# Signs for the projections in four wide instructions, a routing head in three planned pieces, float32 products in parts of two

## The chip, the core and the metric

One core of a Trainium2 chip runs the whole program. The metric is the device time of one launch in microseconds; the figure that counts is the median of several launches. TensorE is called PE here, VectorE DVE, ScalarE ACT, GpSimd POOL, and SyncE, which issues most of the DMAs, SP.

## What is computed

Three layers follow one another on 1536 tokens of width 512.

1. Attention with hashed buckets: for 2 batches of 8 heads, 768 positions of 64 numbers, the signs of `q @ proj` and `k @ proj` (six columns) give each row a bucket, and a query sees only the keys of its own bucket.
2. A mixture of 8 experts with a capacity of 192 tokens each. All (token, expert) logits are taken in falling order, and a token goes to the first expert that still has room. An expert is `relu(x @ w1) @ w2`.
3. A dense layer `silu(x @ w_in) @ w_out` with 2048 hidden columns.

```
for idx in order:                       # logits in falling order
    tok, e = idx // E, idx % E
    if assigned[tok] >= 0 or counts[e] >= cap: continue
    assigned[tok] = e; counts[e] += 1
h = maximum(x[mask] @ w1[e], 0);  out[mask] = h @ w2[e]
```

## The kernel before

**The order of the work.** The instructions of each of the two stages (attention; experts and dense layer) are not written down in their order of execution. Each step is an `op` with an engine, a modelled duration, the steps it depends on and a key; `Plan.run` (L38) then builds a list schedule. It always takes the step that can start first in its model, and among equal starts the one with the lowest key. A step may be held back if a step whose key is lower by more than `gap` would become ready before it ends (less `tol`). Two steps of one engine that depend on each other are put 0.13 us apart in the model (`SLAT`), and in the second stage a step of PE that waits for another engine is planned 0.8 us later than it could start. Every engine then runs its list strictly in that order, so an instruction that waits holds up all that stands behind it on its engine. A change of any modelled duration, or of how a step is cut, can give another order.

**The start.** `lp` (L139) loads `proj` into both halves of `p32`; `pl` (L142) splits it into a rounded part and a rest (`phi`, `plo`), adds the negated copies and puts sixteen blocks of 64 x 6 into `PL`, whose other elements POOL has set to zero (L138). `PL` is the stationary operand of the matmuls of L232, which give the bits of both q and k in one PSUM bank. The other steps of the start are the transposes of q and k (L198, PE), the rounded part of the result (L201, ACT) and the rest (L203, DVE). On POOL stand the memsets of the head buffers (L160 to L162).

**The routing.** The experts close one after another, so there are eight phases. In each, `head` of `route` (L603) finds each token's best open expert; seven calls of `count` (L573) then narrow down the logit at which the next expert is full: compare on DVE (`cmp`, L578), count on PE (`rp`, L582), compare with the room left (`ok`, L585), spread on PE (L588), reduce on DVE (L589). `fin` and `cnt` close the phase. `slots` (L698) then numbers the rows of the expert that closed: `s0` (the expert's number), `f0` (L712, ends with `tot`), `p0` on PE (`rpp`, L726), one-hot rows (`oh`, L735), matmuls that turn them into token numbers (`rpi`, L745), and a gather of 192 rows by POOL (L753) that are transposed on PE (L760). The chain of the next phase and `slots` of the phase just closed compete for the same DVE. The steps of the first four phases have keys below all others.

**The products.** The first six experts that close use their float32 weights as they come (`whole`, L812): a product of four or eight matmuls, planned as steps of four matmuls (1.28 us each in the model). The last two experts and the dense layer use rounded parts and rests (`product`, `second`). The dense layer works on groups of two experts, so its first products (L883) need both experts of the first group.

**The conversion.** The weights of the dense layer come as 64-bit words (`Weights.plan`, L452); 32 blocks are converted with one step on ACT and DVE steps `c1` (two instructions, L467 and L468, planned as one step of 0.8 us), `c2` (L469) and `c3` (L470, on POOL for half of them).

Of the kernel before, what the change touches and what calls it, by code (L numbers as in the profile page):

```python
# [97 lines left out]
def attention(ctx, tc, q, k, v, proj, wg, L, ident, xd, npairs, MW, KC):  # L98
# [34 lines left out]
    V.tensor_scalar(mag,rf[:,1:2],-BIG,1.0,op0=ALU.mult,op1=ALU.add)  # L133
    p32=c1.tile([128,6],F32,name="p32"); wgs=c1.tile([128,4,8],F32,name="wgs")

    phi=c1.tile([128,2,6],F32R,name="phi"); plo=c1.tile([128,2,6],F32R,name="plo")
    PL=c1.tile([128,2,2,128],F32R,name="PL")
    G.memset(PL.bitcast(F32),0.0)  # L138
    def lp():  # L139
        for h in range(2): nc.sync.dma_start(p32[64*h:64*h+64],proj)  # L140
# [285 lines left out]
FP = 6  # L426
# [14 lines left out]
class Weights:  # L441
# [10 lines left out]
    def plan(self, P, a, b, key, pool, ring, after=lambda m: []):  # L452

        nc=self.nc; V=nc.vector; raw={}
        for m in range(a,b):
            n,h=divmod(m,2); c=n//2
            def load(m=m,n=n,h=h,c=c):
                r=raw[m]=pool.tile([128,512,2],I32,name=ring,tag=ring)
                if n%2==0: src=self.wi[h*256:(h+1)*256,c*256:(c+1)*256].rearrange("(a p) f t -> p a (f t)",p=128)
                else: src=self.wo[c*256+h*128:c*256+h*128+128].rearrange("(a p) d t -> p a (d t)",p=128)  # L460
                nc.sync.dma_start(r.rearrange("p (a b) t -> p a (b t)",a=2-n%2),src)
            def t(n=n,h=h): return self.W[n][:,h*512:(h+1)*512]
            def c0(m=m,n=n,h=h,t=t):
                if h==0: self.W[n]=self.res.tile([128,1024],F32,name=f"w{n}")
                nc.scalar.activation(t(),raw[m][:,:,1].bitcast(F32),AF.Abs)
            def c1(t=t):
                V.tensor_scalar(t(),t(),LOW,HIGH,op0=ALU.max,op1=ALU.min)  # L467
                V.tensor_scalar(t().bitcast(I32),t().bitcast(I32),3,0x3FFFFFFF,op0=ALU.logical_shift_left,op1=ALU.bitwise_and)  # L468
            def c2(m=m,t=t): V.scalar_tensor_tensor(t().bitcast(I32),raw[m][:,:,1],-0x40000000,t().bitcast(I32),op0=ALU.bitwise_and,op1=ALU.bitwise_or)  # L469
            def c3(m=m,t=t): V.scalar_tensor_tensor(t().bitcast(I32),raw[m][:,:,0],29,t().bitcast(I32),op0=ALU.logical_shift_right,op1=ALU.bitwise_or)  # L470
            def c4(m=m): l=raw[m][:,:,0]; nc.scalar.activation(l,l.bitcast(U32),AF.Copy,scale=2.0**-29)
            def c5(m=m,t=t): nc.gpsimd.tensor_tensor(t().bitcast(I32),t().bitcast(I32),raw[m][:,:,0],op=ALU.add)
            k=key+m
            P.op(("c64",m),"SP",.45,load,after(m),k,ring,dma=2.3)
            P.op(("cv",m,0),"Activation",.53,c0,[("c64",m)]+([("cv",m-1,0)] if h else []),k)
            P.op(("cv",m,1),"DVE",.8,c1,[("cv",m,0)],k)
            P.op(("cv",m,2),"DVE",.61,c2,[("cv",m,1)],k)
            if m in C3P:
                P.op(("cv",m,4),"Activation",.53,c4,[("c64",m)],k)
                P.op(("cv",m,3),"Pool",1.35,c5,[("cv",m,2),("cv",m,4)],k,frees=[("c64",m)])  # L480
            else: P.op(("cv",m,3),"DVE",.61,c3,[("cv",m,2)],k,frees=[("c64",m)])
# [39 lines left out]
def moe(ctx, tc, L, xd, w1, w2, MW, K, ident, out):  # L521
# [78 lines left out]
    def route(ph):  # L600
        last=ph==7
        ch=Chain(("R",ph),[] if ph==0 else [T_["end",ph-1]])
        def head():  # L603
            eq=rt.tile([128,12,8],F32,name="eq",tag="eq")
            M=T_["M"]=rt.tile([128,12],F32,name="M",tag="M"); mr=rt.tile([128,12],F32,name="mr",tag="mr")
            if ph==0:
                V.tensor_scalar(Lc,L,-1e36,0.0,op0=ALU.max,op1=ALU.add); Lm=Lc
            else:
                pen=rt.tile([128,8],F32,name="pen",tag="pen")
                V.tensor_scalar(pen,T_["cnt"],CAP-0.5,NEG,op0=ALU.is_ge,op1=ALU.mult)  # L610
                Lm=rt.tile([128,12,8],F32,name="Lm",tag="Lm")
                V.tensor_tensor(Lm,Lc,b8(pen),op=ALU.add)
            V.tensor_reduce(M,Lm,axis=AX.X,op=ALU.max)
            V.tensor_tensor(eq,Lm,b12(M),op=ALU.is_equal)
# [7 lines left out]
            V.tensor_tensor(T_["Bw",ph],eq,b12(mr),op=ALU.is_equal)  # L622
        T_["Bw",ph]=None
        ch("DVE",2.7 if ph else 1.6,head)
        if not last:
# [72 lines left out]
    def slots(ph):  # L698
# [56 lines left out]
        for h in range(2):  # L755
# [12 lines left out]
            op(("xt",ph,h),"PE",.5,xt,[("g",ph,0),("g",ph,1)]+([("w1",ph-2,7,1 if ph-2>=FP else 0)] if ph>1 else []),rk(ph)+h*.01,"rp")  # L768
            op(("xh",ph,h),"Activation",.38,xh,[("xt",ph,h)],rk(ph)+h*.01,frees=[("xt",ph,h)])
# [42 lines left out]
    def whole(nm,u,w,xs,n,key,deps):  # L812

        def part(k):
            if k==0: T_["ps",nm]=psm.tile([128,512],F32,name="mm",tag="mm")
            for i in range(k,k+4): nc.tensor.matmul(T_["ps",nm][:,:192],w(i),xs(i),start=i==0,stop=i==n-1)  # L816
        d=deps
        for k in range(0,n,4):
            nn=(*nm,k//4); op(nn,"PE",1.28,lambda k=k: part(k),d,key,"mm" if k==0 else None,frees=[("ld",u)] if k==n-4 else ()); d=[nn]
        return (*nm,0),nn  # L820
    def expert(ph):
        gi=GROUPS.index(grp[ph]); g=grp[ph]; o_=g.index(ph)
        for c in range(4):
            u=("w1",ph,c); key=KEY[u]
            weights(u,lambda t,c=c: nc.sync.dma_start(t.rearrange("p (d f) -> p d f",d=4),w1[bass.ds(regs[ph],1),:,c*256:(c+1)*256].rearrange("o (d p) f -> p (o d) f",p=128)),[("reg",ph)]+([("hi",("w2",ph-1,3))] if ph else []),key,ph>=FP)
            for o in range(2):
                fb=2*c+o; nm=("w1",ph,fb)
                W=lambda i,j,u=u: T_["w",u][j].rearrange("p (d f) -> p d f",d=4)[:,i]
                dp=T_["wn",u]+[("xl",ph,0),("xl",ph,1)]+([("w2",ph-1,d,3 if ph>FP else 1) for d in range(4)] if ph else [])
                if ph<FP:  # L830
# [140 lines left out]
```

## Time and profile before

| | us |
|---|---|
| median of three launches | 857.82 (857.62 to 860.12) |
| launch that was profiled | 856.91 |
| its span in the profile | 854.8 |
| PE busy in the span | 765.5 (90%) |
| DVE busy in the span | 586.4 (69%) |
| mean granted clock of PE | 0.929 of full speed |

The span runs from the first instruction to the last; 2.1 us of the launch lie around it. Attention takes up to about 280 us, the routing of the first expert and its gather up to 322, experts and dense layer the rest. A busy time is that of the records of an engine; in the chain of waits each step is followed back to what released it. One float32 matmul of L816 shows as two records, so a step of four is x8 there.

### The profile page before, as it was taken

How to read it: one execution, taken by the hardware profiler on the slowest of the kernel's cores; microseconds unless marked ns; L12 is line 12 of the kernel's file. 1: busy time of each engine (PE TensorE's matmuls, PEld its weight loads, DVE VectorE, ACT ScalarE, POOL GpSimd, SP SyncE). 2: the span in 40 equal slices, each digit the busy share in tenths (PEclk: the TensorE clock that was granted, in tenths of full speed). 3: DMA queues.
4: the chain of work that ended last, by engine and by line, in shares of the span. 5: the costliest groups of instructions: out<-in, count | busy, mean ns of one | idle time of the engine just before them, and what ended most of it. 6: DMA issues, size and time to landing. Idle time of an engine off the chain costs nothing.

```text
span 854.8 us, 16202 instructions
## 1 busy us (share of the span) xinstructions
PE 765.5 (90%) x6165; PEld 671.2 (79%) x6165; DVE 586.4 (69%) x1432; ACT 418.6 (49%) x805; POOL 385.4 (45%) x276
## 2 busy tenths in 40 slices
PE   4898998999987349697999998999999999999996
PEld 2787877878876238577788897798799899999995
DVE  6768899688785676958796888557357366765441
ACT  2578797888887002123443343423233465655342
POOL 4267588687888010003342344423123455456442
PEclk9679999999999558779999998999999999999998
DMA  8949547565500045554235564122222422301000
GB/s 199 222 127 213 147 123 174 118 157 119 135 2 20 20 166 150 170 167 149 80 114 166 173 197 143 62 75 75 67 72 77 149 75 78 94 2 38 1 1 37
DMA packets 103293, 93.00 MB, mean 109 GB/s; under 512 B 29768, under 2 KB 89160, under 8 KB 103216
## 3 DMA queue, kind: packets, MB, share of 16 engines
q1 hardware_dynamic: 101232, 85.68, 36.2%
q0 software_dynamic: 1984, 6.29, 2.2%
q8 instruction: 48, 0.79, 0.4%
q14 instruction: 29, 0.24, 0.1%
HBM read 66.08 MB, written 6.29 MB: 85 GB/s over the span
## 4 chain that ended last, share of the span: by engine, by line
PE 72%; DVE 19%; issue 4%; ACT 2%; DMA 1%; POOL 1%; POOLq 0%; SPq 0%; DVEq 0%; ACTq 0%
PE mm L883 16%; PE acc L907 14%; PE mm L816 13%; PE S L300 4%; PE rp L582 3%; PE ST L340 3%; PE mm L803 3%; PE ST L341 2%; PE pm L232 2%; PE px L760 2%; DVE S L302 2%; PE mm L804 2%; PE av L362 2%; DVE m L304 1%; PE av L364 1%
## 5 line engine op out<-in xcount | busy, mean ns | idle before, releaser
L350 POOL TENSOR_TENSOR AH<-Aa,AH 128x768 f16<-128x768 f32 x94 | 159.5, 1713 | 78.5 <-ACT AH L348 55.5
L786 POOL TENSOR_TENSOR wlo<-w,whi 128x512 fp32r<-128x512 f32 x68 | 108.0, 1592 | 165.6 <-ACT whi L784 144.1
L883 PE MATMUL mm<-Y,whi 128*128 128x384 f32 x512 | 104.1, 344 | 0.4 <-ACT gh L892 0.4
L345 ACT ACTIVATE Aa<-ST 128x384 f32<-128x384 f32 x192 | 88.2, 496 | 28.1 <-PE ST L341 26.1
L784 ACT CAST whi<-w 128x1024 fp32r<-128x1024 f32 x64 | 67.0, 1050 | 51.0 <-PE acc L907 39.5
L883 PEld LDWEIGHTS mm<-Y,whi 128*128 128x128 f32 x512 | 88.2, 188 | 2.0 <-ACT gh L892 0.5
L300 PE MATMUL S<-k,q 76*128 76x384 f32 x192 | 74.9, 411 | 12.8 <-DVE m L304 5.9
L348 ACT CAST AH<-Aa 128x768 f16<-128x768 f32 x96 | 80.0, 835 | 0.8
L893 DVE TENSOR_TENSOR gl<-sg,gh 128x384 fp32r<-128x384 f32 x64 | 56.9, 891 | 34.0 <-ACT gh L892 33.9
L907 PE MATMUL acc<-whi,gh 128*128 128x512 f32 x192 | 80.0, 417 | 0.0
L816 PE MATMUL mm<-H,wraw 128*128 128x192 f32 x384 | 73.6, 344 | 3.6 <-DVE Y L866 3.6
L786 DVE TENSOR_TENSOR wlo<-w,whi 128x512 fp32r<-128x512 f32 x60 | 50.5, 843 | 36.6 <-ACT whi L784 26.7
L907 PE MATMUL acc<-whi,gl 128*128 128x512 f32 x192 | 75.5, 393 | 0.0
L907 PE MATMUL acc<-wlo,gh 128*128 128x512 f32 x192 | 75.3, 392 | 0.0
L816 PE MATMUL mm<-xhl,wraw 128*128 128x192 f32 x384 | 74.6, 346 | 0.0
L340 PE MATMUL ST<-q,k 128*128 128x384 f32 x192 | 71.7, 373 | 1.7 <-ACT Aa L345 1.7
L889 ACT ACTIVATE sg<-mm 128x384 f32<-128x384 f32 x64 | 31.6, 493 | 81.9 <-PE mm L883 74.5
L816 PEld LDWEIGHTS mm<-H,wraw 128*128 128x128 f32 x384 | 66.2, 199 | 6.0 <-DVE Y L866 3.7
L582 PEld LDWEIGHTS <-cmp 128*63 128x63 bf16 (+2 forms) x588 | 32.2, 126 | 47.0 <-DVE cmp L578 30.7
L341 PE MATMUL ST<-q,k 97*128 97x384 f32 x192 | 67.3, 351 | 0.7 <-ACT q L325 0.6
L753 POOL DMA_INDIRECT xg<-xd,TI x16 | 18.2, 1138 | 107.5 <-DVE TI L748 63.6
L816 PEld LDWEIGHTS mm<-xhl,wraw 128*128 128x128 f32 x384 | 65.3, 199 | 0.6
(252 smaller groups left out, 1836.6 us busy)
## 6 DMA issues: line engine op xcount, KB each, us to landing
wraw<-in_moe_w_dram SPq DMA_DIRECT2D x64, 512.0 KB
craw<-in_moe_w_in_dram SPq DMA_DIRECT2D x14, 512.0 KB
craw<-in_moe_w_out_dram SPq DMA_DIRECT2D x14, 512.0 KB
q<-qh SPq DMA_DIRECT2D x31, 192.0 KB
k<-kh SPq DMA_DIRECT2D x15, 384.0 KB
kn<-in_k_dram SPq DMA_DIRECT2D x16, 192.0 KB
qn<-in_q_dram SPq DMA_DIRECT2D x16, 192.0 KB
vn<-in_v_dram SPq DMA_DIRECT2D x8, 384.0 KB
```

The costliest lines, as they stand in the source:

```text
L300: nc.tensor.matmul(SX[y][:,:384],qq[:76,0,s],kk_[:76,0,s2],start=True,stop=True)
L340: nc.tensor.matmul(ps[:,:384],kk_[:,1,s],qq[:,1,s2],start=True,stop=False)
L341: nc.tensor.matmul(ps[:,:384],kk_[:97,0,s],qq[:97,0,s2],start=False,stop=True)
L345: A_.activation(T_["A",g][:,m],T_["ST",u][:,:384],AF.Exp,scale=0.125)
L348: if e=="Activation": A_.copy(o[:,:,0],T_["A",g])
L350: def lo(e,g=g): (G if e=="Pool" else V).tensor_sub(T_["AH",g][:,:,1],T_["A",g],T_["AH",g][:,:,0])
L582: for b in range(6*h,6*h+6): nc.tensor.matmul(T_[k][:n,:8],cmp[h][:,b-6*h,:],T_["Bw",ph][:,b,:],start=b==0,stop=b==11)
L784: A_.copy(T_["w",u][0],get())
L786: s=slice(h*512,h*512+512); (G if e=="Pool" else V).tensor_sub(T_["w",u][1][:,s],get()[:,s],T_["w",u][0][:,s].bitcast(F32))
L816: for i in range(k,k+4): nc.tensor.matmul(T_["ps",nm][:,:192],w(i),xs(i),start=i==0,stop=i==n-1)
L883: nc.tensor.matmul(T_["ps",nm][:,:384],W(d,int(k==2)),T_["Y",gi][int(k==1)][:,d,:],start=k+d==0,stop=k==2 and d==3)
L907: nc.tensor.matmul(T_["acc",gi,t],a[:,s],x[:,o,:],start=c+o==0 and n==0,stop=c==7 and o==1 and n==2)
```

## The change

- The projections: `phi` and `plo` go, and so do the sixteen small copies. `p32` is now 32 columns wide, zeroed on POOL; the loads fill its first six columns, and a copy repeats them in the next six. A new tile `SG` of 128 x 256 holds +1, -1 or 0; POOL fills it with a memset of zero and eight memsets of 64 x 6. `PL` comes from `SG` times `p32` (into `PF`), a rounding copy, and a subtraction. The memset of `PL` goes.
- The head of a routing phase becomes three steps of the planner with the same instructions in the same order among themselves.
- `c1` of the conversion becomes two steps of one instruction each (0.4 us each in the model).
- `whole` is planned in steps of two matmuls (0.65 us each). Two dependencies that named the last step of such a product by its number are adapted.

```
-    p32=c1.tile([128,6],F32,name="p32"); wgs=c1.tile([128,4,8],F32,name="wgs")
-    phi=c1.tile([128,2,6],F32R,name="phi"); plo=c1.tile([128,2,6],F32R,name="plo")
-    PL=c1.tile([128,2,2,128],F32R,name="PL")
-    G.memset(PL.bitcast(F32),0.0)
+    p32=c1.tile([128,32],F32,name="p32"); wgs=c1.tile([128,4,8],F32,name="wgs")
+    PL=c1.tile([128,2,2,128],F32R,name="PL"); PF=c1.tile([128,2,128],F32,name="PF"); SG=c1.tile([128,2,128],F32,name="SG")
+    G.memset(p32,0.0); G.memset(SG,0.0)
+    for h in range(2):
+        for m in range(2):
+            o=64*h+32*(1-m)
+            for g in range(2): G.memset(SG[64*h:64*h+64,m,o+6*g:o+6*g+6],1.0 if (g+1-m)%2==0 else -1.0)
...
     def pl():
-        V.tensor_copy(phi[:,0],p32); V.tensor_sub(plo[:,0],p32,phi[:,0].bitcast(F32))
-        for x in (phi,plo): V.tensor_scalar(x[:,1],x[:,0].bitcast(F32),-1.0,None,op0=ALU.mult)
-        for m in range(2):
-            for n,x in enumerate((phi,plo)):
-                for h in range(2):
-                    rs=slice(64*h,64*h+64); o=64*h+32*(1-m)
-                    for g in range(2): V.tensor_copy(PL[rs,m,n,o+6*g:o+6*g+6],x[rs,(g+1-m)%2].bitcast(F32))
+        V.tensor_copy(p32[:,6:12],p32[:,:6])
+        V.tensor_tensor(PF.rearrange("p m (b c) -> p (m b) c",c=32),SG.rearrange("p m (b c) -> p (m b) c",c=32),p32[:,None,:].to_broadcast([128,8,32]),op=ALU.mult)
+        V.tensor_copy(PL[:,:,0],PF); V.tensor_sub(PL[:,:,1],PF,PL[:,:,0].bitcast(F32))
...
-op("pl","DVE",1.6,pl,["lp"],-100)
+op("pl","DVE",1.3,pl,["lp"],-100)
...
-            P.op(("cv",m,1),"DVE",.8,c1,[("cv",m,0)],k)
-            P.op(("cv",m,2),"DVE",.61,c2,[("cv",m,1)],k)
+            P.op(("cv",m,1),"DVE",.4,c1,[("cv",m,0)],k)
+            P.op(("cv",m,5),"DVE",.4,c6,[("cv",m,1)],k)
+            P.op(("cv",m,2),"DVE",.61,c2,[("cv",m,5)],k)
...
-        def head():
+        def h1():        # pen, Lm, M            (L610 to L613)
+        def h2():        # eq, eq, mr            (L614 to L616)
+        def h3():        # mr, cthr, cthr, Bw    (L618 to L622)
...
-        ch("DVE",2.7 if ph else 1.6,head)
+        ch("DVE",.7 if ph else .45,h1); ch("DVE",.75 if ph else .7,h2); ch("DVE",.75 if ph else .25,h3)
...
-            for i in range(k,k+4): nc.tensor.matmul(T_["ps",nm][:,:192],w(i),xs(i),start=i==0,stop=i==n-1)
+            for i in range(k,k+2): nc.tensor.matmul(T_["ps",nm][:,:192],w(i),xs(i),start=i==0,stop=i==n-1)
-        for k in range(0,n,4):
-            nn=(*nm,k//4); op(nn,"PE",1.28,lambda k=k: part(k),d,key,"mm" if k==0 else None,frees=[("ld",u)] if k==n-4 else ()); d=[nn]
+        for k in range(0,n,2):
+            nn=(*nm,k//2); op(nn,"PE",.65,lambda k=k: part(k),d,key,"mm" if k==0 else None,frees=[("ld",u)] if k==n-2 else ()); d=[nn]
```

## Rows read from the trace of the kernel before

**Rows 1.** Windows from 349.8 us: length, busy (count) PE, PEld, DVE, ACT, POOL; clock, DMA, GB/s
```profile
349.80:368.70 18.90, 9.89 (x98) 6.98 (x96) 15.20 (x61) 2.60 (x6) 1.95 (x2) 0.61 0.60 187
368.70:393.50 24.80, 24.06 (x152) 22.42 (x153) 18.30 (x47) 8.27 (x17) 5.09 (x5) 0.88 0.53 164
393.50:403.60 10.10, 6.24 (x55) 5.33 (x53) 8.24 (x34) 1.13 (x3) 2.48 (x3) 0.83 0.35 120
403.60:840.00 436.40, 431.32 (x2651) 383.54 (x2650) 277.69 (x645) 188.77 (x356) 175.77 (x115) 0.99 0.28 86
```

**Rows 2.** Windows, the first 20 us
```profile
0.00:20.00 20.00, 8.47 (x30) 6.14 (x30) 12.10 (x42) 5.26 (x11) 10.25 (x24) 0.99 0.85 198
```

**Rows 3.** Chain of waits in the first 20 us: start, length, what
```profile
7.60 0.35 DVE phi L143
...
12.44 0.57 DVE kl L203
...
13.05 0.90 PE pm L198 x3
```

**Rows 4.** Timeline of the first 14 us: start, length, engine, line, operation
```profile
1.33 0.51 POOL L138 MEMSET PL<- 128x512 f32 x1
...
1.93 0.80 DVE L150 CAST identR<-ident 128x128 fp32r<-128x128 f32 x1
...
3.56 1.58 SPq L140 DMA_DIRECT2D p<-in_proj_dram  x2
...
6.50 0.73 POOL L160 MEMSET k<- 64x768 f32 x1
...
7.97 0.17 DVE L143 TENSOR_TENSOR plo<-p,phi 128x6 fp32r<-128x6 f32 x1
...
11.05 0.32 POOL L162 MEMSET vh<- 128x12 f16 x4
```

**Rows 5.** Groups by form on DVE, first 20 us: busy, mean ns, idle before
```profile
L149 DVE CAST PL<-phi 64x6 fp32r<-64x6 f32 x8 | 1.9, 408 | 0.1
```

**Rows 6.** Timeline of PE, 323 to 336 us, with the idle time before
```profile
323.58 2.93 PE L816 MATMUL mm<-xhl,wraw 128*128 128x192 f32 x8
...
330.13 0.18 PE L588 MATMUL rp<-ok,unit 63*128 63x8 bf16 x1
330.23 2.87 PE L816 MATMUL mm<-xhl,wraw 128*128 128x192 f32 x16
...
333.51 1.57 PE L816 MATMUL mm<-xhl,wraw 128*128 128x192 f32 x8
```

**Rows 7.** Timeline of DVE, 346 to 357 us
```profile
348.12 0.26 DVE L614 TENSOR_TENSOR eq<-Lm,M 128x96 f32<-128x96 f32 x1
...
349.52 0.25 DVE L714 TENSOR_TENSOR fm<-A,newc 128x96 f32<-128x96 f32 x1
...
350.31 0.16 DVE L720 CAST tot<-g 128x1 bf16<-128x1 f32 x1
350.38 0.54 DVE L578 TENSOR_TENSOR cmp<-M,th 128x378 bf16<-128x378 f32 x1
...
352.17 0.62 DVE L735 TENSOR_SCALAR oh<-slot,g 128x192 f16<-128x192 bf16 x3
...
355.02 0.23 DVE L639 TENSOR_TENSOR th<-sh,P 128x63 int32<-128x63 int32 x1
```

**Rows 8.** Timeline of DVE, 388 to 398 us
```profile
391.17 1.22 DVE L614 TENSOR_TENSOR eq<-Lm,M 128x96 f32<-128x96 f32 x1
...
396.09 0.24 DVE L714 TENSOR_TENSOR fm<-A,newc 128x96 f32<-128x96 f32 x1
...
396.87 0.16 DVE L720 CAST tot<-g 128x1 bf16<-128x1 f32 x1
```

**Rows 9.** Timeline of POOL, 388 to 398 us
```profile
390.99 4.98 POOL L786 TENSOR_TENSOR wlo<-w,whi 128x512 fp32r<-128x512 f32 x4 [2.23 <-ACT whi L784]
```

**Rows 10.** Timeline of PE, 345 to 400 us
```profile
397.08 0.16 PE L726 MATMUL rpp<-tot,before 128*128 128x1 bf16 x1 [3.57 <-DVE tot L720]
...
397.82 2.30 PE L816 MATMUL mm<-H,wraw 128*128 128x192 f32 x8
```

More of the change, by code (lines that the diff above doesn't have):

```diff
@@ L133, in attention @@
     V.tensor_scalar(mag,rf[:,1:2],-BIG,1.0,op0=ALU.mult,op1=ALU.add)
-    p32=c1.tile([128,6],F32,name="p32"); wgs=c1.tile([128,4,8],F32,name="wgs")
-    phi=c1.tile([128,2,6],F32R,name="phi"); plo=c1.tile([128,2,6],F32R,name="plo")
-    PL=c1.tile([128,2,2,128],F32R,name="PL")
-    G.memset(PL.bitcast(F32),0.0)
+    p32=c1.tile([128,32],F32,name="p32"); wgs=c1.tile([128,4,8],F32,name="wgs")
[5 more added lines that the diff above has]
+            for g in range(2): G.memset(SG[64*h:64*h+64,m,o+6*g:o+6*g+6],1.0 if (g+1-m)%2==0 else -1.0)
     def lp():
-        for h in range(2): nc.sync.dma_start(p32[64*h:64*h+64],proj)
+        for h in range(2): nc.sync.dma_start(p32[64*h:64*h+64,:6],proj)
     def lg(): nc.sync.dma_start(wgs,wg.rearrange("(c p) e -> p c e",p=128))
     def pl():
-        V.tensor_copy(phi[:,0],p32); V.tensor_sub(plo[:,0],p32,phi[:,0].bitcast(F32))
-        for x in (phi,plo): V.tensor_scalar(x[:,1],x[:,0].bitcast(F32),-1.0,None,op0=ALU.mult)
-        for m in range(2):
-            for n,x in enumerate((phi,plo)):
-                for h in range(2):
-                    rs=slice(64*h,64*h+64); o=64*h+32*(1-m)
-                    for g in range(2): V.tensor_copy(PL[rs,m,n,o+6*g:o+6*g+6],x[rs,(g+1-m)%2].bitcast(F32))
+        V.tensor_copy(p32[:,6:12],p32[:,:6])
+        V.tensor_tensor(PF.rearrange("p m (b c) -> p (m b) c",c=32),SG.rearrange("p m (b c) -> p (m b) c",c=32),p32[:,None,:].to_broadcast([128,8,32]),op=ALU.mult)
+        V.tensor_copy(PL[:,:,0],PF); V.tensor_sub(PL[:,:,1],PF,PL[:,:,0].bitcast(F32))
     identR=c1.tile([128,128],F32R,name="identR"); V.tensor_copy(identR,ident)
@@ L174, in attention @@
     op("c0","DVE",3.0,lambda: None,(),-1e4); op("cA","Activation",6.6,lambda: None,(),-1e4)
-    op("lp","SP",1.3,lp,(),-199.0,dma=.1); op("lg","SP",.63,lg,["lp",("t","q",0,1)],KA,dma=.3); op("pl","DVE",1.6,pl,["lp"],-100)
+    op("lp","SP",1.3,lp,(),-199.0,dma=.1); op("lg","SP",.63,lg,["lp",("t","q",0,1)],KA,dma=.3); op("pl","DVE",1.3,pl,["lp"],-100)
     def w0(): A_.activation(wa,wgs.rearrange("p c e -> p (c e)"),AF.Abs,accum_out=wm[:,0:1])
@@ L602, in route @@
         ch=Chain(("R",ph),[] if ph==0 else [T_["end",ph-1]])
-        def head():
-            eq=rt.tile([128,12,8],F32,name="eq",tag="eq")
-            M=T_["M"]=rt.tile([128,12],F32,name="M",tag="M"); mr=rt.tile([128,12],F32,name="mr",tag="mr")
+        H={}
+        def h1():
+            M=T_["M"]=rt.tile([128,12],F32,name="M",tag="M")
             if ph==0:
-                V.tensor_scalar(Lc,L,-1e36,0.0,op0=ALU.max,op1=ALU.add); Lm=Lc
+                V.tensor_scalar(Lc,L,-1e36,0.0,op0=ALU.max,op1=ALU.add); H["L"]=Lc
             else:
@@ L610, in head @@
                 V.tensor_scalar(pen,T_["cnt"],CAP-0.5,NEG,op0=ALU.is_ge,op1=ALU.mult)
[L611 to L614, printed above, removed]
+                H["L"]=rt.tile([128,12,8],F32,name="Lm",tag="Lm")
+                V.tensor_tensor(H["L"],Lc,b8(pen),op=ALU.add)
+            V.tensor_reduce(M,H["L"],axis=AX.X,op=ALU.max)
+        def h2():
+            eq=H["eq"]=rt.tile([128,12,8],F32,name="eq",tag="eq"); mr=H["mr"]=rt.tile([128,12],F32,name="mr",tag="mr")
+            V.tensor_tensor(eq,H["L"],b12(T_["M"]),op=ALU.is_equal)
             V.tensor_tensor(eq,eq,b8(w8),op=ALU.mult)
             V.tensor_reduce(mr,eq,axis=AX.X,op=ALU.max)
+        def h3():
+            mr=H["mr"]
             if ph>0:
@@ L828, in expert @@
                 W=lambda i,j,u=u: T_["w",u][j].rearrange("p (d f) -> p d f",d=4)[:,i]
-                dp=T_["wn",u]+[("xl",ph,0),("xl",ph,1)]+([("w2",ph-1,d,3 if ph>FP else 1) for d in range(4)] if ph else [])
+                dp=T_["wn",u]+[("xl",ph,0),("xl",ph,1)]+([("w2",ph-1,d,3) for d in range(4)] if ph else [])
                 if ph<FP:
```

9 lines of the change are left out of this document (4 added, 5 removed).

## The prediction

> **What bounds the kernel now.** I read the busy times by windows first, because PE's share of the whole span (90%) hides that the stages have different limits. From 403.6 to 840 us PE is busy 431.3 of 436.4 us [rows 1]: there the amount of matmul work alone sets the end, and the change takes none of it away. What it can save lies in stretches where PE waits. The windows show three that the change touches: the start, where PE works 8.5 of 20 us [rows 2]; 349.8 to 368.7, where it works 9.9 of 18.9 us, partly at a granted clock of one half; and 393.5 to 403.6, 6.2 of 10.1 us [rows 1]. Whatever is saved ahead of 403.6 us moves the saturated stretch, and so the end, by as much, unless the order changes for the worse.
>
> The chain of waits says why PE waits at the start: from 7.60 to 12.44 us it runs through the instructions of the projections on DVE, after which come the rest of k (L203) and, at 13.05, the next transposes [rows 3]. For the two later stretches I read the timelines of PE and DVE side by side. PE there has run out of products of the expert at hand, and the next expert can only start after routing, slots, gather and transposes. So the routing chain is what bounds 322 to 403 us: each thing that delays it counts.
>
> **Part 1, the projections.** Removed from the chain: 12.44 - 7.60 = 4.84 us [rows 3], twenty instructions, sixteen of them copies, of which the eight of the rounded part have records of 408 ns on average [rows 5]. Added: four instructions. None of them has a row of its own, so I bound them. Cheapest: 0.17 us for the 6-column copy, like the 6-column subtraction [rows 4], and for each 256-column instruction something between the 96 columns of L614 (0.26 us) [rows 7] and the 384 columns of L203 (0.57 us) [rows 3], about 0.42 us; together 0.17 + 3 x 0.42 = 1.4 us. Dearest: POOL is busy with its memsets of 0.73 us until 11.4 us [rows 4], and beside POOL's work a DVE instruction can take much longer: the same 96-column L614 took 0.26 us without and 1.22 us with POOL at work [rows 7 to 9], 0.96 us more. If all four pay that, 1.4 + 4 x 0.96 = 5.3 us, and the part loses 0.4 us. Of the rows at the place itself, the 128-column copy of L150 took 0.80 us and the 6-column subtraction 0.17 us beside memsets [rows 4]: some pay and some don't. I take the 1.4 us and one delay of that size, 2.3 us, and so a gain of 2.5 us (ends: 3.4 gained, 0.4 lost).
>
> The trace shows a DVE instruction with two inputs in SBUF at four times its length beside POOL [rows 8, 9], but a small one at its usual length [rows 4]. The Trainium skill (GPSIMD Engine Reference, Specifications) says that POOL's SBUF interface is shared with VectorE and that instructions with two SBUF inputs, or in a two-port mode, contend. By that all four new instructions would be exposed, and the sum would be the dear end. The trace bears it out for L614 and not for L143, so it stands below as a rival and not in the sum.
>
> On POOL the memset of PL (0.51 us) goes, and p32, SG and eight small ones come. By columns SG costs half of it, 0.26 us, and nine small ones at 0.32/4 = 0.08 us [rows 4] cost 0.72: POOL's later memsets end about 0.5 us later. Their cover is that the first head needs its buffers only after the bits, which come later than 13 us. There is one new wait: the load of proj, and all SP issues behind it, waits for the memset of p32. That stands where the memset of PL stood, at 1.33 us, and the load is issued at 3.56 [rows 4]: more than 1.5 us of cover, so nothing. The DMA engines are busy 0.85 of the first 20 us [rows 2]; the chain goes through no DMA between 7.6 and 14 us, so I count the gain in full here, and its loss to the DMA as part of the range.
>
> **Part 2, products in parts of two.** A round of the routing has two trips from PE to DVE and back. In the round from 330.13 to about 335.1 us PE does 2.8 us of products (x16, two steps of four) between the spread and the count, and 1.5 us (x8) between the count and the next spread [rows 6]. The round takes 4.9 us. DVE's part of the long trip is a threshold of 0.23 us and a compare of 0.54 us [rows 7], with the reduce and the gaps some 1.3 us by my estimate, so PE comes back more than a microsecond late. With steps of half the size the planner can end the filling one half step sooner: 2.1 instead of 2.8 us, 0.7 us a round. Three rounds of the second phase have this form (those that begin at 330, 335 and 340 us): 2.1 us at most. Against it: at half clock one step of four takes 2.9 us [rows 6], and the planner, which reckons with full clock, may put three small ones there, 4.3 us. I take 1.8 us for the start of the second expert (ends: 2.1 gained, 1.4 lost). The number of matmuls does not change, and in the saturated stretch a finer order neither adds nor removes work: zero, with 2 us either way for another order.
>
> **Part 3, the head.** Near 348 us DVE does the ten instructions of the next phase's head in one go, and only then f0 of the slots: L614 to L622 take 348.12 to 349.52 us, after which fm to tot take 0.95 us [rows 7]. With three steps the planner sees f0 ready when the first ends, while the second is ready 0.13 us later in its model, and takes f0. So tot, and with it the numbering, the gather and the second expert, come 349.52 - 348.12 = 1.4 us sooner. The third expert's slots gain more: there L614 to L622 last from 391.17 to 396.09, 4.9 us, since POOL works beside them [rows 8, 9], and PE, whose list has rpp ahead of the last products of that expert, stands for 3.57 us [rows 10]. f0 ahead of them will meet the same work of POOL: its fm and its tot may each pay 0.96 us, so tot comes 4.9 - 2 = 2.9 us sooner; I take 2.5 us off PE's wait (ends: 3.57 and 0). What is late next is the head itself: it, and the next phase's first compare, come 0.95 us later behind f0. Part of that is on the path, and I put 1.0 us against the sum. If the shorter wait also spares the half clock behind it (x8 in 2.3 us instead of 1.5 [rows 10], twice), 1.6 us more would be gained; not counted.
>
> **Part 4, the conversion.** No instruction is added. A step of 0.4 us fits into gaps where 0.8 did not; it can make a chain step on DVE wait by up to a piece, or bring weights sooner. Weights aren't what ends PE's waits here, so I count nothing (0.5 us either way per phase that counts, two of them).
>
> **The sum.** Second expert 1.8 + 1.4 = 3.2 us sooner; PE is busy 24.1 of the 24.8 us from 368.7 to 393.5 [rows 1], so that the end of that expert moves along. Then 2.5 us off the next wait, and 1.0 back: 4.7 us. With the start: 4.7 + 2.5 = 7.2 us. The profiled launch took 856.91 us (its span of 854.8 and 2.1 around it), so 849.7 us. The median of the runs is 0.9 us above that launch: 850.6.
>
> **The rivals.**
> 1. *The wide instructions wait for POOL.* All four pay the 0.96 us, and the start gains nothing: 4.7 us, 853.1 us. For it: L614 and L150. Against it: L143, and that copies of six columns got along with 0.41 us [rows 5]. Chance 0.15. By the rule of the Trainium skill (GPSIMD Engine Reference, Specifications) this would be the main case.
> 2. *The planner does not use the finer steps on the path.* The routing is bounded by what the 0.8 us of extra distance on PE demands, PE's wait moves to the next semaphore, and only the start stays: 2.5 us, about 855.3 us. For it: the short trip has exactly one step of four where that distance asks for 1.28 us, and two small steps fill the same. Chance 0.15; half of it within 0.3%.
> 3. *Slower: the slots overtake the routing.* Once the head is cut, not only f0 but also the four one-hot steps (twelve instructions, 4 x 0.62 = 2.5 us [rows 7]) and the conversions go ahead of its second and third piece. The phase is then late by 0.95 + 2.5 = 3.4 us, and that twice, for the third and the fourth expert, in a stretch where PE has no other work: 6.9 us, and if the start gains its 2.5, 4.4 us net: 862.2 us. It decides from the point where the expert at hand ends before the next routing phase does; that is so at 349.8 and 393.5 us [rows 1]. Against it: the one-hot steps need PE's rpp first, about a microsecond in which the head can go on. Chance 0.15.
>
> **How the numbers follow.** The forecast has the remaining 0.55, with 844 to 854 as its own range: the sum of the good ends (3.4 + 2.1 + 1.4 + 3.6 + 1.6, about 12) is not likely to come all at once, nor that of the bad ones. A measurement of this kernel can tell 0.3%, 2.6 us, from no change: below 855.2 is faster, above 860.4 slower. Faster: 0.55 + 0.15 + 0.07 = 0.77. Same: the other half of rival 2 and the lower edge of rival 3, 0.11. Slower: 0.12. The range goes from 843, a little under the forecast's own, to 860, where about a tenth is left out on either side.
>
> **What would show it.** In the profile after, DVE has four instructions of the projections within 2 to 2.5 us of 7.6, and the transposes that began at 13.05 begin near 10.5. In the timeline of DVE L714 stands ahead of L614 in the second and third phases. Between spread and count PE does about 2.1 us of products. PE's wait ahead of rpp is about 1 us, and the first L883, at 403.6 now, comes near 396. The prediction is wrong if attention ends no sooner than now, if the head is still in one piece on DVE, or if the first L883 moves by less than the start does.

## The result, and the profile after

| | before | after |
|---|---|---|
| median of four launches, us | 858.38 (857.62 to 860.12) | 849.91 (844.59 to 852.11) |
| ratio, 95% interval | | 0.9889 (0.9841 to 0.9938) |
| launch that was profiled, us | 856.91 | 849.9 |
| its span, us | 854.8 | 848.1 |
| mean granted clock of PE | 0.929 | 0.931 |

The kernel is 1.1% faster (0.6 to 1.6%); the forecast was 850.6. (Times and ratios here are of launches within 1.5% of their kernel's fastest; four of the twelve of `no_h`, at 864.0 to 865.0 us and a mean clock of 0.920, its traced one among them, lie beyond.) In the two traced launches the 6.7 us of span lie at these places: the first float32 product (L816, now L819) begins at 322.0 us instead of 323.6; from there to the second expert's first product it is 41.0 us instead of 45.6; from there to the first matmul of the dense layer (L883, now L886) 33.8 instead of 34.4; the rest takes as long as before. The windows after, with the same columns as [rows 1, 2]; the second runs from the end of the first expert's products to the first product of the second:

```profile
0.00:20.00 20.00, 10.55 (x36) 8.05 (x36) 11.82 (x32) 5.32 (x12) 10.36 (x33) 0.94 0.92 201
348.20:362.90 14.70, 8.15 (x96) 6.01 (x95) 12.95 (x48) 2.11 (x5) 2.04 (x2) 0.63 0.68 218
362.90:388.50 25.60, 25.57 (x171) 23.92 (x170) 20.73 (x53) 9.81 (x20) 4.72 (x4) 0.95 0.53 168
388.50:396.70 8.20, 2.61 (x38) 2.09 (x37) 7.78 (x39) 1.60 (x2) 0.33 (x1) 0.78 0.77 251
396.70:832.80 436.10, 432.91 (x2649) 383.61 (x2648) 276.60 (x643) 188.06 (x354) 172.39 (x117) 0.99 0.27 85
```

The stretch without products of the second expert went from 19.4 to 14.7 us (the window in [rows 1], 18.9, ends half a microsecond ahead of that expert's first product at 369.17), with 6.55 instead of 9.1 us of idle PE; the stretch ahead of the dense layer from 10.1 to 8.2 us, but with 5.6 instead of 3.9 us of idle: that one is shorter because less work is left in it. The saturated stretch is as long as it was (436.1 against 436.4 us).

From the first float32 product to the last of the dense layer's first products (L883, now L886) it is 510.7 us instead of 515.7; this stretch is called the expert stage below, as in the expectations. Of these 5.0 us, 2.8 are idle time of PE (15.9 instead of 18.7). In the other 2.2 PE is busy for less time with the same matmuls: 19.9 instead of 26.2 us of its work there ran at the half clock of 1.2 GHz. The second part does not come with the order alone: `c_late` below runs the same list behind the first product, has the same idle time (15.8 us), 28.1 us at half clock, and takes 513.4 us.

The start, answering [rows 3, 4], from the timeline of the kernel after (start, length, engine, line, operation):

```profile
1.92 0.21 DVE L149 CAST identR<-ident 128x128 fp32r<-128x128 f32 x1
...
7.31 0.73 POOL L159 MEMSET q<- 64x768 f32 x1
7.63 0.44 DVE L146 COPY p<-p 128x6 f32<-128x6 f32 x1
...
8.10 0.73 POOL L160 MEMSET k<- 1x768 f32 x1
8.18 0.42 DVE L147 TENSOR_TENSOR PF<-SG,p 128x256 f32<-128x256 f32 x1
8.63 0.35 DVE L148 CAST PL<-PF 128x256 fp32r<-128x256 f32 x1
8.89 0.77 POOL L159 MEMSET k<- 64x768 f32 x1
9.02 0.43 DVE L148 TENSOR_TENSOR PL<-PF,PL 128x256 fp32r<-128x256 f32 x1
9.36 0.55 DVE L202 TENSOR_TENSOR kl<-pm,kh 128x384 fp32r<-128x384 f32 x1
...
9.97 0.90 PE L197 MATMUL pm<-ident,qn 128*128 128x128 f32 x3 [1.30 <-DVE kl L202]
```

The four instructions take 9.36 - 7.63 = 1.73 us in place of 4.84, and the transposes behind them begin 3.08 us sooner. The two with two inputs (8.18 and 9.02) run at 0.42 and 0.43 us although a memset of POOL runs beside each.

DVE around the slots of the second and of the third expert, answering [rows 7, 8]:

```profile
344.28 0.25 DVE L717 TENSOR_TENSOR fm<-A,newc 128x96 f32<-128x96 f32 x1
...
345.06 0.16 DVE L723 CAST tot<-g 128x1 bf16<-128x1 f32 x1
345.13 0.25 DVE L615 TENSOR_TENSOR eq<-Lm,M 128x96 f32<-128x96 f32 x1
...
386.49 1.15 DVE L708 TENSOR_SCALAR closed<-cnt 128x8 f32<-128x8 f32 x1
...
389.36 0.25 DVE L717 TENSOR_TENSOR fm<-A,newc 128x96 f32<-128x96 f32 x1
...
390.14 0.16 DVE L723 CAST tot<-g 128x1 bf16<-128x1 f32 x1
390.21 0.25 DVE L615 TENSOR_TENSOR eq<-Lm,M 128x96 f32<-128x96 f32 x1
```

Both times `fm` to `tot` now stand ahead of `eq`. From the copy that opens `slots` (`cnt`, L695, now L698, at 342.31 and 386.07) to `tot` it is 2.75 us instead of 3.9, and 4.1 instead of 7.5. PE around `rpp`, answering [rows 10]:

```profile
346.65 0.17 PE L729 MATMUL rpp<-tot,before 128*128 128x1 bf16 x1
...
390.35 0.16 PE L729 MATMUL rpp<-tot,before 128*128 128x1 bf16 x1 [1.89 <-DVE tot L723]
392.68 0.35 PE L581 MATMUL rp<-Bw,cmp 128*63 128x8 bf16 x6 [2.17 <-DVE cmp L577]
```

The wait of 3.57 us has become 1.89, and right behind it stands a new one of 2.17 us for the first compare of the next phase. The rounds, answering [rows 6] (L587 is the spread, L581 the count):

```profile
324.81 0.18 PE L587 MATMUL rp<-ok,unit 63*128 63x8 bf16 x1
324.92 2.22 PE L819 MATMUL mm<-xhl,wraw 128*128 128x192 f32 x12
...
329.98 0.18 PE L587 MATMUL rp<-ok,unit 63*128 63x8 bf16 x1
330.09 3.52 PE L819 MATMUL mm<-xhl,wraw 128*128 128x192 f32 x20
...
335.27 0.17 PE L587 MATMUL rp<-ok,unit 78*128 78x8 bf16 x1
335.30 0.90 PE L819 MATMUL mm<-xhl,wraw 128*128 128x192 f32 x4
```

Between spread and count there are x12, x20 and x4 where x16 stood, and the rounds from 324.81 last 5.2, 5.3 and 4.7 us. Before they lasted 4.9, 4.6 and 4.5 (spreads at 330.13, 335.01, 339.64 and 344.18). They are not shorter.

### The profile page after: what moved, and what is told of

It is laid out like the page before. It is cut to its first block, busy times and chain, and to the rows that moved or that the text cites. A ratio compares the mean times of both kernels' runs of the same rounds, so it can differ in the third digit from the quotient of the medians.

```text
span 848.1 us, 16201 instructions
## 1 busy us (share of the span) xinstructions
PE 767.3 (90%) x6165; PEld 673.2 (79%) x6165; DVE 579.5 (68%) x1416; ACT 418.7 (49%) x805; POOL 378.5 (45%) x285
## 4 chain that ended last, share of the span: by engine, by line
PE 68%; DVE 21%; issue 4%; DMA 2%; ACT 2%; POOL 1%; POOLq 0%; SPq 0%; DVEq 0%; ACTq 0%
PE mm L886 14%; PE acc L910 14%; PE mm L819 12%; PE S L299 4%; PE rp L581 3%; PE ST L339 3%; PE ST L340 3%; PE mm L806 2%; PE pm L231 2%; PE px L763 2%; DVE cmp L577 2%; DVE S L301 2%; PE av L361 2%; PE mm L807 2%; PE av L363 1%
## 5 line engine op out<-in xcount | busy, mean ns | idle before, releaser
L789 POOL TENSOR_TENSOR wlo<-w,whi 128x512 fp32r<-128x512 f32 x68 | 105.2, 1551 | 178.5 <-ACT whi L787 161.0
L886 PE MATMUL mm<-Y,whi 128*128 128x384 f32 x512 | 107.8, 349 | 0.0
L886 PEld LDWEIGHTS mm<-Y,whi 128*128 128x128 f32 x512 | 89.7, 190 | 1.6 <-issue 0.4
L299 PE MATMUL S<-k,q 76*128 76x384 f32 x192 | 74.8, 414 | 12.2 <-DVE S L301 5.8
L896 DVE TENSOR_TENSOR gl<-sg,gh 128x384 fp32r<-128x384 f32 x64 | 54.3, 850 | 34.0 <-ACT gh L895 33.8
L819 PE MATMUL mm<-H,wraw 128*128 128x192 f32 x384 | 76.3, 340 | 0.0
L819 PE MATMUL mm<-xhl,wraw 128*128 128x192 f32 x384 | 75.1, 343 | 0.3 <-ACT H L838 0.3
L789 DVE TENSOR_TENSOR wlo<-w,whi 128x512 fp32r<-128x512 f32 x60 | 53.0, 885 | 31.1 <-ACT whi L787 22.8
L581 PEld LDWEIGHTS <-cmp 128*63 128x63 bf16 (+2 forms) x588 | 32.3, 126 | 43.9 <-DVE cmp L577 27.8
L819 PEld LDWEIGHTS mm<-xhl,wraw 128*128 128x128 f32 x384 | 64.6, 196 | 3.1 <-issue 1.5
L363 PE MATMUL av<-vh,AH 128*128 128x66 f16 x576 | 65.4, 197 | 1.6 <-DVE AH L349 1.1
L361 PE MATMUL av<-vh,AH 128*128 128x66 f16 x576 | 66.7, 201 | 0.0
```

Source lines behind the costliest of these rows:

```text
L299: nc.tensor.matmul(SX[y][:,:384],qq[:76,0,s],kk_[:76,0,s2],start=True,stop=True)
L361: nc.tensor.matmul(a,x[:,0,s],vh[:,h,kt],start=kt==0,stop=False,skip_group_check=True)
L363: nc.tensor.matmul(a,x[:,1,s],vh[:,h,kt],start=False,stop=kt==5,skip_group_check=True)
L789: s=slice(h*512,h*512+512); (G if e=="Pool" else V).tensor_sub(T_["w",u][1][:,s],get()[:,s],T_["w",u][0][:,s].bitcast(F32))
L819: for i in range(k,k+2): nc.tensor.matmul(T_["ps",nm][:,:192],w(i),xs(i),start=i==0,stop=i==n-1)
L886: nc.tensor.matmul(T_["ps",nm][:,:384],W(d,int(k==2)),T_["Y",gi][int(k==1)][:,d,:],start=k+d==0,stop=k==2 and d==3)
```

## The experiments

Three kinds: one part alone, the whole change without one part, and one part only in some of the phases. The times (ratio to the kernel before, launched beside it) are followed by two numbers of the traces, PE's idle time in the first 60 us and in the expert stage. The last column sets the launches of all kernels to one mean clock: within a kernel the time falls by 0.62 us for each 0.001 of mean granted clock (fitted over all of them), and the column gives each kernel's mean at 0.931, with a standard error of 0.1 to 0.7 us.

| kernel | median, us | ratio, 95% | idle, first 60 us | idle, later | at 0.931, us |
|---|---|---|---|---|---|
| before | 856.07 to 858.38 | 1 | 16.3 | 18.7 | 857.1 |
| after | 849.91 | 0.989 (0.984 to 0.994) | 12.0 | 15.9 | 849.8 |
| s_only | 852.28 | 0.9948 (0.9925 to 0.9971) | 12.2 | 18.7 | 851.6 |
| h_only | 857.57 | 1.0020 (1.0003 to 1.0037) | 16.7 | 18.1 | 858.1 |
| p_only | 858.87 | 1.0027 (1.0009 to 1.0045) | 16.7 | 19.1 | 858.4 |
| c_only | 862.91 | 1.0071 (1.0042 to 1.0100) | 16.6 | 22.6 | 861.7 |
| no_s | 854.46 | 0.9955 (0.9936 to 0.9974) | 15.8 | 16.1 | 854.9 |
| no_c | 850.78 | 0.9924 (0.9900 to 0.9948) | 12.0 | 19.0 | 853.6 |
| no_h | 856.63 | 0.9976 (0.9951 to 1.0002) | 12.0 | 20.0 | 855.7 |
| no_p | 849.88 | 0.9925 (0.9898 to 0.9952) | 12.1 | 20.2 | 854.3 |
| h_ph1 | 852.09 | 0.9965 (0.9941 to 0.9989) | 12.1 | 17.4 | 852.1 |
| h_rest | 856.01 | 0.9981 (0.9958 to 1.0005) | 12.8 | 18.0 | 853.6 |
| p_late | 848.41 | 0.9915 (0.9882 to 0.9948) | 12.2 | 17.8 | 851.0 |
| c_late | 848.26 | 0.9901 (0.9875 to 0.9928) | 12.1 | 15.8 | 849.3 |

Each kernel has one trace. That of no_h is of a launch at a mean clock of 0.920, so only its order and its idle times are used. The last column is a help to rank the kernels, not a measurement of its own: a difference of clock that an order brings about is taken out with the rest. Where it and the medians disagree (no_c, no_p, p_late), the times alone do not decide.

**s_only: the projections alone.** The kernel before with the start of the change.

```
-    phi=...; plo=...; PL=c1.tile([128,2,2,128],F32R,name="PL")
-    G.memset(PL.bitcast(F32),0.0)
+    PL=...; PF=...; SG=...
+    G.memset(p32,0.0); G.memset(SG,0.0)
...
```

> Only the projections are changed (tile of signs, four instructions), all else as before. Theory A (the parts act where they stand and add up): the first matmul of ST comes 3 to 4 us sooner as in the changed kernel, the end of attention 2.5 us sooner, the rest follows unchanged: about 855 us. Rival B (the whole gain of 8 us comes from another order in the routing stage, and the start is eaten up by attention): end of attention within 1 us of before, 857 to 859 us.

Ratio 0.9948: 4.5 us faster (2.5 to 6.4). Its first 60 us have 12.2 us of idle PE, like all nine kernels with the new start (12.0 to 12.8), against 15.8 to 16.7 in the five with the old one. So the start is worth about 4.2 us of idle time, more than the 3.1 at its place; the rest arises behind it, where the order of attention is another too. From the first product on, the kernel is the one before: 516.0 against 515.7 us. So rival B falls, and theory A holds with a larger gain than its 855 us.

**h_only, p_only, c_only: one of the other parts alone.** The kernel before with the three-step head; with the steps of two matmuls; with the two-step conversion.

```
-        ch("DVE",2.7 if ph else 1.6,head)
+        ch("DVE",.7 if ph else .45,h1); ch("DVE",.75 if ph else .7,h2); ch("DVE",.75 if ph else .25,h3)
```

> Only the routing head is cut into three planned pieces. Theory A: f0 of the slots stands ahead of the second piece in the second and third phases, the second expert starts 1.4 us sooner, PE's wait of 3.6 us ahead of rpp in the third phase shrinks by 2 to 3 us, 1 us goes back: 855 us. Rival B (finer parts of the products are what lets the routing come sooner): no change, 857 to 859 us. Rival C (slots overtake the routing): 860 us or more.

```
-            for i in range(k,k+4): nc.tensor.matmul(...)
+            for i in range(k,k+2): nc.tensor.matmul(...)
```

> Only the float32 products are planned in parts of two. Theory A: the rounds of the second phase that hold products shorten by up to 0.7 us each, the second expert starts 1.8 us sooner, 856 us. Rival B (this is the main cause): the second expert starts 4 us or more sooner and the time is 853 us or less. Rival C (the planner's distance on PE binds): 857 to 859 us.

```
-            P.op(("cv",m,1),"DVE",.8,c1,[("cv",m,0)],k)
+            P.op(("cv",m,1),"DVE",.4,c1,[("cv",m,0)],k)
+            P.op(("cv",m,5),"DVE",.4,c6,[("cv",m,1)],k)
```

> Only the first conversion step is planned as two steps of one instruction. Theory A: nothing that ends a wait changes, 857 to 859 us. Rival B (the short steps fill gaps, so that the long conversions no longer stand in the routing's way): the second expert starts a microsecond or more sooner, 855 us. Rival C (they stand in its way more often): 860 us.

None is a gain: the ratios are 1.0020, 1.0027 and 1.0071, all with intervals above 1. Theory A's gain came neither for the head (857.57 us, in rival B's range) nor for the parts of two (858.87, in rival C's), and c_only came out as its rival C (862.91). That refutes the prediction's terms as terms that can be added. The head does bring the second expert sooner by itself (42.9 us behind the first product instead of 45.6), and the dense layer's first matmul is at 396.3 us; but near 516 us the gain is given back. The parts of two bring it later (49.7 us): the products of the first expert run out and PE stands ahead of `rpp`, because the head, in one piece here, is ahead of `tot` on DVE. PE of p_only, two consecutive records:

```profile
347.81 0.90 PE L816 MATMUL mm<-H,wraw 128*128 128x192 f32 x4
352.44 0.16 PE L726 MATMUL rpp<-tot,before 128*128 128x1 bf16 x1 [3.73 <-DVE tot L720]
```

Where h_only and c_only lose most is one place, the numbering of the fifth expert that closes. Four records: PE and DVE of the kernel before, PE of h_only, PE of c_only, in this order.

```profile
522.34 1.01 PE L816 MATMUL mm<-H,wraw 128*128 128x192 f32 x2 [3.57 <-DVE Y L866]
```

```profile
518.27 3.75 DVE L735 TENSOR_SCALAR oh<-slot,g 128x192 f16<-128x192 bf16 x3
```

```profile
521.45 2.93 PE L820 MATMUL mm<-H,wraw 128*128 128x192 f32 x8 [5.58 <-DVE Y L870]
```

```profile
514.89 0.17 PE L726 MATMUL rpp<-tot,before 128*128 128x1 bf16 x1
521.12 0.48 PE L582 MATMUL rp<-Bw,cmp 128*63 128x8 bf16 x6 [6.07 <-DVE cmp L578]
```

In the kernel before and in h_only PE waits for `Y`, which stands on DVE behind one-hot rows that take 3.75 us (2.79 in h_only) for three instead of 0.62 [rows 7]. In c_only PE's list has the count right behind `rpp`, and the compare it needs stands on DVE behind the whole head, the numbering, two steps of one-hot rows and a conversion. In the kernel after, the longest wait of PE between 500 and 540 us is under 1 us. Nothing of the change aims at that place: it is another order.

**no_s, no_c, no_h, no_p: the change without one part.** In each the lines of that part are those of the kernel before.

```
no_s
-    G.memset(p32,0.0); G.memset(SG,0.0)
...
+    G.memset(PL.bitcast(F32),0.0)
...
no_c
-            P.op(("cv",m,1),"DVE",.4,c1,[("cv",m,0)],k)
-            P.op(("cv",m,5),"DVE",.4,c6,[("cv",m,1)],k)
+            P.op(("cv",m,1),"DVE",.8,c1,[("cv",m,0)],k)
no_h
-        ch("DVE",.7 if ph else .45,h1); ch("DVE",.75 if ph else .7,h2); ch("DVE",.75 if ph else .25,h3)
+        ch("DVE",2.7 if ph else 1.6,head)
no_p
-        for k in range(0,n,2):
+        for k in range(0,n,4):
```

> All of the change but the projections, which stay as they were. Theory D (the stage of the experts gains by the three cuts together, and the start gains by itself): from the first float32 product to the last matmul of L886's kind the profile shows 510 us as in the changed kernel (516 before), and the first stage is as before plus what the cut conversion costs attention: 853 to 856 us. Rival A (the parts add up one by one, +0.7, +2 and +6 us as measured alone): 865 us.

> All of the change but the cut conversion step. If the cut conversion costs attention 3 us or more and the expert stage does not need it: 845 to 847 us, faster than the changed kernel, with attention's end 3 us or more sooner than in it. If the expert stage needs it (rival): the stage from the first float32 product on takes 515 us or more instead of 510, and the time is 851 to 855 us.

> All of the change but the cut of the routing head. Theory D (the cuts work together): without the head the expert stage falls back to 515 to 519 us as with each cut alone, 854 to 858 us. Rival A (my terms as predicted): 2.9 us slower than the changed kernel, 852 to 853 us, with L614's kind in one piece ahead of f0 and PE's wait ahead of rpp in the third phase back at 3 us or more.

> All of the change but the parts of two. Theory D: the expert stage falls back to 515 to 519 us, 854 to 858 us. Rival A (my terms as predicted): 1.8 us slower than the changed kernel, about 851.5 us, with 2.8 us of products between spread and count in three rounds of the second phase.

The start adds to the rest: s_only alone gains 4.5 us, no_s (the other three parts together) 3.9 (2.2 to 5.5), and the sum, 8.4, is inside the interval of the whole change (5.3 to 13.6). The other three don't add: alone each loses, each pair (no_c, no_h, no_p) has as much idle time after the first product as the kernel before or more (19.0 to 20.2 against 18.7), and only all three together come down to 16 (15.9, and 16.1 in no_s). The launches show it for the head alone: the interval of no_h (0.9951 to 1.0002) lies above that of the kernel after (0.9841 to 0.9938). Without the conversion or without the parts of two the medians, 850.78 and 849.88 us, cannot be told from 849.91; there only the idle times of single traces and the last column speak for the third part.

Of the expectations, no_s met theory D (854.46 us, expert stage 511.0), and so did no_h in time (856.63). no_c took 518.0 us for the expert stage, as its rival has it, and 850.78 in all, just under the rival's range. no_p took 515.6 us there, as theory D has it, but its 849.88 us lie outside theory D's range and nearer to rival A's 851.5.

PE's waits from 322 us on, summed by what ended them; first the kernel before, then the one after, then no_c (us in total, times, longest):

```profile
PE rp L582 <- DVE cmp L578: 6.1, 7, 2.2
PE rpp L726 <- DVE tot L720: 5.0, 3, 3.6
PE mm L816 <- DVE Y L866: 3.6, 1, 3.6
```

```profile
PE rp L581 <- DVE cmp L577: 7.8, 8, 2.2
PE rp L587 <- DVE ok L584: 3.3, 5, 1.1
PE rpp L729 <- DVE tot L723: 3.2, 2, 1.9
```

```profile
PE rp L581 <- DVE cmp L577: 7.5, 9, 2.1
PE rpp L729 <- DVE tot L723: 3.9, 2, 3.4
PE rpi L748 <- DVE oh L738: 2.6, 3, 1.1
```

Waits for `tot` fall by 1.8 us, the one for `Y` goes, and waits for compares grow by 1.7.

**h_ph1 and h_rest: the three-step head in two phases only, or in the other six.** The rest of the change stays.

```
+        if ph<2:        # h_rest: ph>1
             ch(...,h1); ch(...,h2); ch(...,h3)
+        else: ch("DVE",2.7 if ph else 1.6,lambda: (h1(),h2(),h3()))
```

> The changed kernel with the head cut in the first two phases only, one piece in the six later ones. Where the cut's worth comes from the second phase's head slipping into the gaps of the first slots (theory E), the expert stage keeps most of its gain: 511 to 513 us in the profile, 850 to 852 us, the second expert's products 41 to 43 us after the first's. Where it comes from f0 standing ahead of the head's second piece in every later phase (theory A), the stage falls back toward the 525 us that it takes without any cut: 518 us or more, 855 us or more.

> The changed kernel with the head cut in the six later phases only, one piece in the first two. Theory E (slipping into the gaps of the first slots counts): the second phase's head ends 2 us later than in the changed kernel, one round of the routing less lies ahead of the first product, and the stage takes 515 us or more: 854 us or more. Theory A (f0 ahead counts): 511 to 513 us, 850 to 852 us.

Neither half holds the whole. The expert stage takes 514.6 us in h_ph1 and 519.3 in h_rest, with 510.7 for the kernel after and 513.4 for c_late, which has the same order as it: so the range of 511 to 513 for h_ph1 was missed, its second expert comes 44.5 us behind the first product and not 41 to 43, and the strong form of theory E (all is in the first two phases) falls; h_rest (856.01 us) came out as theory E has it. In idle time of the stage h_ph1 and h_rest (17.4 and 18.0 us) lie between no_h and the whole. At one clock the cut of the first two phases gains 3.6 us over no_h and that of the six others 2.2; the whole cut gains 6.0. By their ratios the three (0.9965, 0.9981, 0.9976) cannot be told apart.

**p_late: parts of four for the first two experts, of two from the third on.**

```
+        st=4 if nm[1]<2 else 2
-        for k in range(0,n,2):
+        for k in range(0,n,st):
```

> The changed kernel with parts of two for the third to the sixth expert only, parts of four for the first two. My term (finer parts shorten the rounds of the second phase): the end of the second phase comes about 2 us later than in the changed kernel and the expert stage takes 512 to 515 us: 851 to 854 us. Rival F (they count only in the stretch where the dense layer's products are there too): the second phase ends no later, the stage takes 510 to 511 us, and PE's idle time from 404 to 540 us stays at 3 us instead of the 9 with parts of four throughout: 849 to 850 us.

The rounds that my term speaks of lie in the first expert, and there this kernel has the old steps. The second expert starts 41.3 us behind the first product (41.0 in the kernel after, 42.6 in no_p), the dense layer 74.4 us behind it (74.8). So the steps of two gain next to nothing up to there. Nor are the rounds shorter with them: from the first product to the `cnt` of the second expert it is 17.8 us here and 19.0 in no_p, but 20.4 in the kernel after and 20.4 and 21.8 in no_s and c_late, which have its order. The expert stage takes 512.2 us, as my term had it but not for its reason, since the second expert is no later. PE's idle time from 404 to 540 us is 6.7 us, between the 9.3 of no_p and the 3.0 of the kernel after, so that rival F's 3 is missed as well, and the median of 848.41 lies below both ranges. What the steps take off the idle time, beside the other parts, lies behind the first two experts.

**c_late: the two-step conversion only in the stage of experts and dense layer**, not in attention.

```
+            if m<NC:
+                P.op(("cv",m,1),"DVE",.8,lambda c1=c1,c6=c6: (c1(),c6()),[("cv",m,0)],k)
```

> The changed kernel with the conversion cut only for the 28 blocks that are converted in the expert stage; the four in attention keep one step of two instructions. If the cut costs attention something (theory G: 3 to 5 us more of half clock in its profiles): the first product comes at 315 to 320 us and the time is 845 to 848 us. If that was chance (rival): 849 to 850 us, the first product at 317 to 322 us. In both the expert stage takes 510 to 511 us.

The first product is at 317.0 us, which both ranges hold; the median, 848.26, lies between theory G's 845 to 848 and the rival's 849 to 850. At one clock the kernel is level with the one after (849.3 and 849.8). And kernels with the same attention order as c_late (s_only, no_c) have that product at 315.4 and 320.2. So the theory isn't shown: chance covers it. What both expected, 510 to 511 us for the expert stage, was missed: it takes 513.4, though every engine runs the same list there as in the kernel after. PE is idle as long (15.8 us), but 28.1 us of its work ran at half clock and not 19.9. So two traces whose expert stage differs by under 3 us do not show a better order by that; the idle time of equal orders agrees to 0.3 us. c_late and p_late are no slower than the kernel after; the two together weren't run.

## Why the prediction came out

**The reading of the bound** held: what was saved ahead of the saturated stretch arrived at the end, and that stretch kept its length.

**The start: right in its mechanism, too small in size.** I took 2.3 us for four instructions and 2.5 of gain. They took 1.73 (only the copy paid a delay, 0.44 us where I had 0.17), the place gained 3.1, and by s_only the whole is worth 4.5 us (2.5 to 6.4). In the traced launch of the kernel after only 1.6 us of it are left at 322 us: PE's idle time until then is 5.5 us less (57.1 against 62.6), but 8.2 us more of its work ran at the half clock of 1.2 GHz (60.4 against 52.2 us), and it was busy 3.9 us longer (264.9 against 261.0). That is a matter of the launch, not of the start (see the last section).

**Rival 1, the wait for POOL, is refuted** for the two wide instructions with two inputs. The row that does show POOL is the copy of six columns: it begins at 7.63, during a memset that runs from 7.31 to 8.04, and ends at 8.07. The cast at 8.63 ends 0.15 us behind the memset of 8.10 to 8.83. The Trainium skill (SBUF — State Buffer, Who interferes with whom) separates the cases: a VectorE instruction with two SBUF inputs contends with a GpSimd instruction that reads SBUF and not with one that only writes, while copies and casts in a two-port mode contend with any. The trace agrees on both: 0.42 and 0.43 us beside memsets, but 1.22 us for `eq` beside POOL's subtraction, which reads [rows 8, 9]. The line that the prediction had cited leaves that distinction out.

**f0 ahead of the head: right.** The second expert's `tot` comes 1.15 us sooner behind `cnt` (1.4 predicted), the third's 3.4 (2.9 predicted). Off the wait ahead of `rpp` went 1.7 us and not 2.5, and the new wait behind it, for the compare, cost 2.2 where I put 1.0 back: in all, the stretch from the second expert's first product to the dense layer got only 0.6 us shorter (33.8 instead of 34.4), where I had 1.5; in c_late, with the same order and more half clock, it is 34.8 us, no shorter than before.

**"With steps of half the size the planner can end the filling one half step sooner": this step failed.** The rounds were not shortened (see p_late as well), and p_only, where nothing else is changed, brings the second expert 4.1 us later. Yet the second expert came 4.6 us sooner in the kernel after and in no_s, against my 3.2 (3.1 in c_late, which has the same order). In place of the rounds stands something that I had at nothing: the head of the second phase. DVE between the closing of the first expert and that phase's first compares, in the kernel after:

```profile
303.51 0.17 DVE L698 COPY cnt<-rpc 128x8 f32<-128x8 f32 x1 [0.26 <-PE rpc L694]
...
305.34 0.16 DVE L609 TENSOR_SCALAR pen<-cnt 128x8 f32<-128x8 f32 x1
...
306.45 2.24 DVE L738 TENSOR_SCALAR oh<-slot,g 128x192 f16<-128x192 bf16 x12
308.61 0.25 DVE L615 TENSOR_TENSOR eq<-Lm,M 128x96 f32<-128x96 f32 x1
...
310.14 0.99 DVE L577 TENSOR_TENSOR cmp<-M,th 128x378 bf16<-128x378 f32 x2
```

And in the kernel before, where that `cnt` stood at 305.23:

```profile
311.26 0.15 DVE L610 TENSOR_SCALAR pen<-cnt 128x8 f32<-128x8 f32 x1
...
313.66 1.01 DVE L578 TENSOR_TENSOR cmp<-M,th 128x378 bf16<-128x378 f32 x2
```

Its first piece runs while PE does `rpp`, the two others while PE does `rpi`; before, the head began only after the slots were through, at 311.26. So the first compare comes 6.63 us behind `cnt` instead of 8.43. All fourteen traces agree on this: 6.6 us in the eight kernels whose head is cut in that phase, 8.4 in the six others. From the first product to the `cnt` of the second expert it is then 20.4 us instead of 22.8, and h_only has this gain without any parts of two (20.2 us; 42.9 against 45.6 us to the second expert). It is also where the one-hot rows overtake two pieces of the head, as in rival 3: it cost nothing there, for PE had `rpi` to do.

**"The conversion: I count nothing" failed as well.** Alone it costs 0.7% (0.4 to 1.0%). Beside the three others it may be worth something: at one clock no_c is 3.8 us behind the kernel after, and its idle time in the expert stage is 19.0 instead of 15.9 us; but the intervals of the two (0.9900 to 0.9948 and 0.9841 to 0.9938) overlap, so the times don't show it.

**The sum.** 2.5 for the start and 4.7 for the rest made 7.2; measured were 4.5 and 3.9. That the total was hit is in good part luck: the start was too small, and the rest is made of other pieces than I named: the head in the second phase, an order without the wait of 3.57 us at 518.8, and in the traced launch 2.2 us from less work at half clock, none of which stood in the sum. Rival 2 (only the start stays, 855.3) describes s_only, and it was half right: the finer products are not used where I wanted them. Why all three parts together escape the waits near 516 us, while each alone and each pair has one there or elsewhere, stays open. That the idle time goes with the order of the list, not with the work, is what equal orders show: 18.7 us twice, 15.8 to 16.1 three times. No run changed the order without a part of the change, so how often another order would do as well by chance isn't known.

## What to carry to other kernels

Where a planner orders the work, price a finer cut only for the stretch where the trace shows who will go ahead of whom, and test it both alone and taken out of the whole: here three cuts lost 0.2 to 0.7% alone and gained 0.45% together. The saving ahead of everything, the start, added up with the rest here, within the intervals. Look at the mean granted clock of each launch before believing differences of a few us.

## What was not expected

**The clock differs between launches of one kernel, by nearly as much as the change is worth.** The ten launches of s_only fall into two groups: 848.6 to 850.6 us at a mean clock of 0.934, and 853.9 to 854.9 us at 0.927. In the traces it shows in attention. The first 280 us of s_only and of no_c, whose attention has the same order:

```profile
0.00:280.00 280.00, 241.10 (x2853) 208.65 (x2853) 218.01 (x465) 208.02 (x404) 194.81 (x157) 0.94 0.57 135
```

```profile
0.00:280.00 280.00, 245.15 (x2840) 212.64 (x2840) 214.48 (x447) 208.20 (x404) 194.47 (x157) 0.92 0.57 135
```

PE is busy 4 us longer in the second for no more work, at a clock of 0.92 against 0.94, and the first product is at 320.2 instead of 315.4 us. Up to that product the traces have 43 to 60 us of PE time at the half clock, and kernels with the same attention order lie at both ends (p_late 44, the kernel after 60). Behind it, two pairs with the same order agree in the length of the expert stage, 515.7 and 516.0 us (before and s_only), 510.7 and 511.0 (after and no_s); c_late, with the order of the second pair, takes 513.4.

**A small cast beside a long memset.** `identR<-ident`, 128 columns, takes 0.79 us in every trace with the old start and 0.22 in every one with the new, where POOL at that time fills `SG` in small pieces. It lies in nobody's way.
